# y of the later MoE spans by seven products of halves, half of the relus on ScalarE

## The chip, the cores and the metric

The kernel runs on one core of a Trainium2 chip. The metric is device time in microseconds (us), the median of several runs: 257.5 us before the change (three runs, 256.58 to 257.63).

## What is computed

Blockwise causal attention over 8 batches, 8 heads, 576 positions and a head dimension of 64, and then, over the 4608 tokens of 512 features that it gives, a layer that takes the larger of two projections:

```python
mask = block_i >= block_j            # blocks of 64 positions
attn = softmax(where(mask, scale * q @ k.T, -1e9))
x = (attn @ v)                       # as 4608 x 512
h1, h2 = x @ w1, x @ w2              # 512 -> 1024
out = maximum(h1, h2) @ w_out        # 1024 -> 512
```

The kernel rewrites the second half with max(h1, h2) = h2 + relu(h1 - h2). With d = w1 - w2 and M = w2 @ w_out it computes g = relu(x @ d) and out = x @ M + g @ w_out. M is formed once, on chip. So y, the output, is a product with a contraction of 1536: 4 chunks of 128 rows from x and M, 8 chunks from g and w_out.

## The kernel before

**Attention** goes by head pairs: two heads share the 128 partitions, four pairs make a batch, 32 pairs in all. For a pair, TensorE forms transposed scores in PSUM (the pool `ps_s`, two buffers of two banks), ScalarE takes the exponential into the tile `aT` (`exp`), POOL writes zeros over the masked corners (`mask`), and two pairs later (`LAG`) TensorE multiplies by v (`av`, output `ps_o`, first the query tiles 0 and 1, then 2 to 4). VectorE divides by the sums (a reciprocal and a multiplication into `xp`). `xp` is transposed into `xT`, mostly by DMA. q is transposed on TensorE (`transposes`, two PSUM tiles, one copied out by VectorE, one by ScalarE); from the seventh group on k is transposed by DMA.

**The MoE layer** goes by spans of tokens: two short ones of the first batch (256 and 320 tokens), seven of 512, and a last one of 448. As the spans from the third on begin 64 tokens off a multiple of 128, a span carries the last 64 columns of g over from the one before (a POOL copy at its first h), and its y covers four whole tiles of 128 tokens. For each span there are 8 units `h_unit(i, f)`, each of 4 matmuls of 512 columns and a relu from PSUM into g on VectorE, and 4 units `y_unit(i, s)`, each of 12 matmuls of 512 columns, a copy from PSUM to the tile `y` on VectorE, and a 256 KB store issued by SP. The last tile of the last span is cut into 256, 128 and 128 columns (`y_last`).

**Order.** The scheduling is manual: each engine executes in the order in which the program is written. `plan()` lists the MoE units, `fill(n)` takes n steps from them (a step is one matmul and, at the end of a unit, what follows it), skipping units whose tokens are not yet there. The main loop goes over groups of two pairs and puts fills between the scores, the attention outputs and the transposes. h, y, attention outputs and all transposes share one PSUM pool, `ps_m`, with four buffers of one bank; a new tile takes the buffer that was let go first, and its first matmul waits for the last reader of the tile before.

From the fourth span on the pattern repeats every four pairs: the 8 h units of a span, then its 4 y units, with the attention of four pairs between. The two q transposes of such a cycle stand one in the y part and one where the next h part begins. The last two spans run at the end with no attention beside them.

Of the kernel before, what the change touches and what calls it, by code (L numbers as in the profile page):

```python
# [8 lines left out]
FP32 = mybir.dt.float32  # L9
BF16 = mybir.dt.bfloat16  # L10
AF = mybir.ActivationFunctionType
# [3 lines left out]
def kernel(  # L15
# [10 lines left out]
    nc = tc.nc  # L26

    B, H, S, D = q.shape
    P = 128
# [3 lines left out]
    d_model = H * D  # L33
# [3 lines left out]
    NTOK = B * S  # L37
# [33 lines left out]
    spans = [(0, QCUT), (QCUT, S - QCUT)]  # L71
    spans += [(t0, min(SPAN, NTOK - t0)) for t0 in range(S, NTOK, SPAN)]
    NSPAN = len(spans)


    carry = [t0 % P for t0, _ in spans]
    tiles = [(carry[i] + w) // P for i, (_, w) in enumerate(spans)]

# [5 lines left out]
    wraw = ctx.enter_context(tc.tile_pool(name="wraw", bufs=4))  # L84
    qkn = ctx.enter_context(tc.tile_pool(name="qkn", bufs=2))
    g_pool = ctx.enter_context(tc.tile_pool(name="g", bufs=2))
    y_pool = ctx.enter_context(tc.tile_pool(name="y", bufs=4))
    ps_s = ctx.enter_context(tc.tile_pool(name="ps_s", bufs=2, space=bass.MemoryType.PSUM))
    ps_m = ctx.enter_context(tc.tile_pool(name="ps_m", bufs=4, space=bass.MemoryType.PSUM))

# [9 lines left out]
    xT = ring.tile([P, NDM, NTOK + BLK], BF16, name="xT")  # L100
    d_sb = wpool.tile([P, NDM, d_ff], BF16, name="d_sb")
    bT_sb = wpool.tile([P, NFF, d_model], BF16, name="bT_sb")
    m_sb = wpool.tile([P, NDM, d_model], BF16, name="m_sb")
    wo_sb = wpool.tile([P, NFF, d_model], BF16, name="wo_sb")
# [5 lines left out]
    dve, pool, act = nc.vector.tensor_copy, nc.gpsimd.tensor_copy, nc.scalar.copy  # L110
# [51 lines left out]
    def load_v(b, c):  # L162
        rows = min(P, S - c * P)
        nc.gpsimd.dma_start(  # L164
            out=vv_r[b % NV][P - rows:, c, :, :D],
            in_=v[b, :, c * P:c * P + rows, :].rearrange("h p d -> p h d"),
        )
# [7 lines left out]
    for j in range(d_ff // WB):  # L175
        row, n = (1, j) if j < 3 else (3, 0)
        t0 = 3 * S - 3 * BLK + n * NDM * WB
# [21 lines left out]
    dve, pool, act = nc.vector.tensor_copy, nc.gpsimd.tensor_copy, nc.scalar.copy  # L199
# [28 lines left out]
    g_tiles = {}  # L228

    def h_unit(i, f):  # L230
        if f == 0:
            g_tiles[i] = g_pool.tile([P, NFF, SPAN + BLK], BF16, name="g")
            if carry[i]:
                end = carry[i - 1] + spans[i - 1][1]
                nc.gpsimd.tensor_copy(  # L235
                    out=g_tiles[i][:, :, :carry[i]],
                    in_=g_tiles[i - 1][:, :, end - carry[i]:end])
        g = g_tiles[i]
        t0, w = spans[i]
        m = carry[i]  # L240
        pt = ps_m.tile([P, SPAN], FP32, name="ps_h", tag="m")
        for c in range(NDM):
            nc.tensor.matmul(  # L243
                pt[:, :w], d_sb[:, c, f * P:(f + 1) * P], xT[:, c, t0:t0 + w],
                start=(c == 0), stop=(c == NDM - 1),
            )
            if c == NDM - 1:
                nc.vector.tensor_scalar_max(g[:, f, m:m + w], pt[:, :w], 0.0)  # L248
            yield

    def bT_unit(j):
        pt = ps_m.tile([P, 2, NDM, P], BF16, name="ps_bT", tag="m")
        for i in range(2):
            for c in range(NDM):
                nc.tensor.transpose(pt[:, i, c, :], w2_sb[j][:, c, i * P:(i + 1) * P], ident[:])
                if i == 1 and c == NDM - 1:
                    (act if j % 2 else dve)(
                        out=bT_sb[:, 2 * j:2 * j + 2, :],
                        in_=pt.rearrange("p i c d -> p i (c d)"))
                yield  # L260
# [19 lines left out]
    def y_unit(i, s):  # L280
        t0 = spans[i][0] - carry[i] + s * P
        py = ps_m.tile([P, d_model], FP32, name="ps_y", tag="m")
        terms = y_terms(i, s)
        for n, (lhs, rhs) in enumerate(terms):
            nc.tensor.matmul(  # L285
                py[:], lhs, rhs, start=(n == 0), stop=(n == len(terms) - 1),
            )
            if n == len(terms) - 1:
                y = y_pool.tile([P, d_model], FP32, name="y")
                nc.vector.tensor_copy(out=y[:], in_=py[:])  # L290
                nc.sync.dma_start(out=out[t0:t0 + P, :], in_=y[:])
            yield

    def y_last(i, s):
        t0 = spans[i][0] - carry[i] + s * P
        for m, w, copy, queue in ((0, 256, act, SP), (256, P, dve, SP), (384, P, act, ACT)):
            py = ps_m.tile([P, w], FP32, name="ps_y", tag="m")
            terms = y_terms(i, s)
            for n, (lhs, rhs) in enumerate(terms):
                nc.tensor.matmul(  # L300
                    py[:], lhs, rhs[:, m:m + w], start=(n == 0), stop=(n == len(terms) - 1),
                )
                if n == len(terms) - 1:
                    y = y_pool.tile([P, d_model], FP32, name="y")
                    copy(out=y[:, :w], in_=py[:])  # L305
                    queue.dma_start(out=out[t0:t0 + P, m:m + w], in_=y[:, :w])
                yield


    units = []  # L310
    NY = NDM + NFF

    def plan():
        def h(i, f):
            t0, w = spans[i]
            units.append((h_unit(i, f), t0 + w, w / SPAN, NDM))

        def y(i, s, last=False):
            t0, w = spans[i]
            if last:  # L320
                units.append((y_last(i, s), t0 + w, 0.333, 3 * NY))
            else:
                units.append((y_unit(i, s), t0 + w, 1.0, NY))

        for i in range(NSPAN):
            for f in range(NFF):
                h(i, f)
                if i == 0 and f % 2:
                    units.append((bT_unit(f // 2), 0, 0.25, 2 * NDM))
                if i > 2 and f % 2 == 0 and f // 2 < tiles[i - 1]:  # L330
                    y(i - 1, f // 2)
            if i == 1:
                for n in range(2 * NDM):
                    units.append((m_unit(n // NDM, n % NDM), 0, 0.5, NFF))
                for j in range(2):
                    for s in range(tiles[j]):
                        y(j, s)
        n = tiles[-1]
        for s in range(n):
            y(NSPAN - 1, s, s == n - 1)  # L340

    plan()
    todo = [[n, u, need, cost] for u, need, cost, n in units]
# [225 lines left out]
    def pool_work(s):  # L569
        g, i = divmod(s, 2)  # L570
        if s == 4:
            load_qk(4, (SP, SP), gated=True)
        elif s == 5:
            load_qk(5, (SP, SP), gated=True)
            cast("q", 4, ((pool, 0, RPP),))
            cast("k", 4, ((pool, 0, RPP),))
        else:
            if i == 1 and g + 3 < NG:
                load_qk(g + 3, (SP, SP), gated=True)
            if i == 1 and g + 2 < NG:  # L580
                cast("q", g + 2, ((pool, 0, RPP),))
                cast("k", g + 2, ((pool, 0, RPP),))
            nb, j = divmod(s + 2, HP)
            if nb < B:
                for c in ((0, 1), (2, 3), (4,), ())[j]:
                    load_v(nb, c)
            for nm in "qk":
                if i == 1 and g + 3 < NG and by_dma(nm, g + 3):
                    load_blocks(nm, g + 3)
# [112 lines left out]
    n = fill_of(GPB)  # L702
# [10 lines left out]
    for g in range(GPB + 1, NG):  # L713
        a, b = 2 * g, 2 * g + 1
        old = done_tokens[0]
        if x_due:
            x_out(x_due.pop())
        n, new = fill_of(g), done_tokens[0]
        region(tile_0(a), tile_1(a))
        lo, hi = max(3, n // 18), n * 2 // 9  # L720
        for p, tiles in ((a, lambda: (tile_2(a), tile_0(b))), (b, lambda: (tile_1(b), tile_2(b)))):
            done_tokens[0] = old if p == a and x_by_dma(g - 2) else new
            fill(hi)
            av_with(p - LAG, lo)
            done_tokens[0] = new
            if p % 2 and x_by_dma(g - 1):
                x_dma(g - 1)
            if p % 2 == 0:
                for nm in "qk":
                    if g + 1 < NG and by_dma(nm, g + 1):  # L730
                        transpose_blocks(nm, g + 1)
            copy_out = t_pair(p)
            outs = tiles()
            copy_out()
            region(*outs)
            if p % 2 and g + 1 < NG:
                pad_keys(p + 1)
                pad_keys(p + 2)
            pool_work(p)
        x_due.append(g - 1)  # L740
        fill(n - 2 * (lo + hi))
    for p in range(NPAIR - LAG, NPAIR):
# [48 lines left out]
```

## Time and profile before

| | |
|---|---|
| median of the runs | 257.5 us (256.58 to 257.63) |
| span of the profiled execution, first to last instruction | 255.8 us |
| around the span, by the median | 1.7 us |
| the profiled execution's own time | not listed; the page gives its span |
| mean granted TensorE clock | 1.000 |
| TensorE busy | 245.8 us |
| VectorE busy | 149.9 us |
| ScalarE busy | 120.1 us, none between about 204 and 250 us |
| POOL busy | 128.0 us |
| h matmuls, 320, and y matmuls, 280 + 140 + 36 | 68.3 us and 70.6 + 38.1 us and the end |
| chain that ended last, share of TensorE | 86% |

A group in the profile is a line of the kernel, an engine, an operation and the tiles that it writes and reads, with its count, its busy time, the mean duration of one, and the idle time of the engine in front of it. Matmuls overlap in their pipeline, so the duration of one is longer than the time from one start to the next; the busy time of a group is the union of its instructions.

### The profile page before, as it was taken

The page shows a single profiled execution, that of the slowest core. Times are in us where ns is not written, and L with a number is a line of the kernel's source. Part 1 is how long each engine was busy: PE and PEld are TensorE (multiplying, and loading weights), DVE is VectorE, ACT ScalarE, POOL GpSimd, SP SyncE. Part 2 cuts the span into 40 slices and gives each one's busy share as a digit, 9 for nine tenths or more (in the row PEclk, how much of TensorE's full clock was granted, in tenths as well). Part 3 has the DMA queues.
Part 4 walks back from the last instruction along what each step waited for, and adds up shares of the span by engine and source line. Part 5 has one row for each costly group of instructions (what it writes and reads, how often), then busy time and mean ns, then how long its engine had stood idle before and what let it go on. Part 6 is the DMA issues. An engine that isn't in the chain of part 4 may idle for free.

```text
span 255.8 us, 6863 instructions
## 1 busy us (share of the span) xinstructions
PE 245.8 (96%) x2803; PEld 136.5 (53%) x2803; DVE 149.9 (59%) x320; ACT 120.1 (47%) x159; POOL 128.0 (50%) x294
## 2 busy tenths in 40 slices
PE   8699999899999999999999999999999999999994
PEld 2346767765555555555555555555555554444443
DVE  4876986656576447644764476457544864664521
ACT  2788864477565555555555555555555400000000
POOL 1986951588869457845784578557331200000000
PEclk9999999999999999999999999999999999999999
DMA  6999999599999999999999999999952301202122
GB/s 240 316 222 308 190 265 229 191 127 175 171 144 231 154 219 147 214 138 232 161 197 153 218 166 219 151 216 160 118 103 85 85 23 70 85 0 82 66 100 84
DMA packets 104384, 41.29 MB, mean 161 GB/s; under 512 B 89248, under 2 KB 93728, under 8 KB 104352
## 3 DMA queue, kind: packets, MB, share of 16 engines
q0 software_dynamic: 65952, 11.87, 60.9%
q1 hardware_dynamic: 37984, 28.32, 48.4%
q10 hardware_dynamic: 416, 0.66, 0.8%
q8 instruction: 22, 0.36, 0.7%
q14 instruction: 10, 0.08, 0.1%
HBM read 34.60 MB, written 9.44 MB: 172 GB/s over the span
## 4 chain that ended last, share of the span: by engine, by line
PE 86%; DMA 6%; POOL 3%; ACT 2%; DVE 1%; issue 1%; SPq 0%; POOLq 0%
PE ps_y L285 37%; PE ps_h L243 22%; PE ps_o L507 10%; PE ps_s L399 8%; PE ps_w L369 4%; DMA kraw<-in_k_dram 3%; DMA qraw<-in_q_dram 3%; PE ps_qT L380 2%; PE ps_M L266 1%; ACT aT L423 1%; PE ps_y L300 1%; POOL kn L160 1%; PE ps_s L417 1%; POOL wo_sb L196 1%; PE ps_xe L545 1%
## 5 line engine op out<-in xcount | busy, mean ns | idle before, releaser
L423 ACT ACTIVATE aT<-ps_s 128x1024 bf16<-128x1024 f32 (+2 forms) x100 | 95.7, 994 | 46.1 <-PE ps_s L399 34.2
L285 PE MATMUL ps_y<-wo_sb,g 128*128 128x512 bf16 x280 | 70.6, 380 | 0.0
L243 PE MATMUL ps_h<-xT,d_sb 128*128 128x512 bf16 (+3 forms) x320 | 68.3, 358 | 0.3 <-DVE d_sb L190 0.3
L248 DVE TENSOR_SCALAR g<-ps_h 128x512 bf16<-128x512 f32 (+3 forms) x80 | 50.7, 637 | 17.5 <-PE ps_h L243 15.2
L428 POOL MEMSET aT<- 64x128 bf16 x124 | 22.0, 199 | 60.9 <-ACT aT L423 59.8
L290 DVE COPY y<-ps_y 128x512 f32<-128x512 f32 x35 | 24.2, 692 | 45.9 <-PE ps_y L285 45.0
L243 PEld LDWEIGHTS <-d_sb 128*128 128x128 bf16 x320 | 29.5, 98 | 30.1 <-issue 2.3
L507 PEld LDWEIGHTS <-aT 128*128 128x128 bf16 x960 | 37.2, 98 | 13.5 <-issue 0.8
L285 PEld LDWEIGHTS <-g 128*128 128x128 bf16 x280 | 24.9, 98 | 30.7 <-issue 5.3
L507 PE MATMUL ps_o<-vv,aT 128*128 128x65 bf16 x960 | 39.8, 194 | 0.0
L285 PE MATMUL ps_y<-m_sb,xT 128*128 128x512 bf16 x140 | 38.1, 379 | 0.0
L164 POOL DMA_DIRECT2D vv<-in_v_dram x40 | 34.0, 857 | 1.3 <-issue 0.9
L399 PE MATMUL ps_s<-qT,kT 64*128 64x64 bf16 (+6 forms) x344 | 31.2, 280 | 1.6 <-ACT kT L388 0.7
L514 DVE TENSOR_TENSOR xp<-ps_o,rec 128x256 bf16<-128x256 f32 (+1 forms) x64 | 31.4, 491 | 2.2
L137 POOL DMA_DIRECT2D kb<-in_k_dram x40 | 29.4, 759 | 0.0
L513 DVE RECIPROCAL rec<-ps_o 128x4 f32<-128x4 f32 (+1 forms) x64 | 11.9, 186 | 23.7 <-PE ps_o L507 23.5
L305 ACT COPY y<-ps_y 128x256 f32<-128x256 f32 (+1 forms) x2 | 0.6, 318 | 48.4 <-PE ps_y L300 48.4
L388 ACT COPY qT<-ps_qT 128x576 bf16<-128x576 bf16 (+1 forms) x17 | 10.3, 613 | 27.2 <-PE ps_qT L380 27.2
L160 POOL CAST qn<-qraw 128x1152 bf16<-128x1152 f32 (+1 forms) x16 | 17.0, 1061 | 8.4 <-DMA qraw<-in_q_dram 8.4
L285 PEld LDWEIGHTS <-xT 128*128 128x128 bf16 x140 | 12.8, 98 | 13.1 <-issue 0.4
L399 PEld LDWEIGHTS <-kT 64*128 64x128 bf16 x344 | 12.0, 94 | 11.6 <-issue 6.2
L235 POOL COPY g<-g 128x512 bf16<-128x512 bf16 x8 | 4.9, 613 | 22.4 <-DVE g L248 22.1
(58 smaller groups left out, 152.1 us busy)
## 6 DMA issues: line engine op xcount, KB each, us to landing
qraw<-in_q_dram SPq DMA_DIRECT2D x16, 576.0 KB, 4.9
out_dram<-y SPq DMA_DIRECT2D x35, 256.0 KB, 4.1
vv<-in_v_dram POOLq DMA_DIRECT2D x32, 128.0 KB, 5.6
kraw<-in_k_dram SPq DMA_DIRECT2D x5, 576.0 KB, 7.5
kb<-in_k_dram POOLq DMA_DIRECT2D x40, 72.0 KB, 6.4
w1raw<-in_moe_w_dram POOLq DMA_DIRECT2D x4, 512.0 KB, 7.4
xT<-in_moe_w_dram POOLq DMA_DIRECT2D x4, 256.0 KB, 7.9
wo_sb<-in_moe_w_out_dram POOLq DMA_DIRECT2D x2, 512.0 KB, 10.2
```

What stands on the lines that cost most here:

```text
L137: nc.gpsimd.dma_start(out=n[h * BLK:(h + 1) * BLK, :, s], in_=(q if nm == "q" else k)[b, 4 * u + 2 * s + h].rearrange("(j p) d -> p j d", ...
L160: copy(out=n[:, j0:j1], in_=t[:, j0:j1])
L164: nc.gpsimd.dma_start(out=vv_r[b % NV][P - rows:, c, :, :D], in_=v[b, :, c * P:c * P + rows, :].rearrange("h p d -> p h d"),)
L243: nc.tensor.matmul(pt[:, :w], d_sb[:, c, f * P:(f + 1) * P], xT[:, c, t0:t0 + w], start=(c == 0), stop=(c == NDM - 1),)
L248: nc.vector.tensor_scalar_max(g[:, f, m:m + w], pt[:, :w], 0.0)
L285: nc.tensor.matmul(py[:], lhs, rhs, start=(n == 0), stop=(n == len(terms) - 1),)
L290: nc.vector.tensor_copy(out=y[:], in_=py[:])
L399: nc.tensor.matmul(ps[:, hh, col:col + w], kT[r, k0:k0 + P], qT[r, q0:q0 + w], start=True, stop=True,)
L423: nc.scalar.activation(out=aT_r[p % NA][:, :, a0:a0 + w], in_=ps[:, :, :w], func=AF.Exp, scale=scale,)
L428: (eng or nc.gpsimd).memset(aT_r[p % NA][BLK:, :, a0:a0 + BLK], 0.0)
L507: nc.tensor.matmul(po[:, gi, hh, :], a[:, hh, a0:a0 + P], vv[:, c, h0 + 2 * hh, :], start=(mm == 0), stop=(mm == n_mm - 1),)
L514: nc.vector.tensor_mul(xp[:, :, ts[0]:ts[0] + n, p % 2].rearrange("q s t d -> q t s d"), po[:, :, :, :D], rec[:, :n].to_broadcast([P, n, 2 ...
```

## The change

From the fourth span on (`i >= FAST`, `FAST = 3`) the four y tiles of a span are no longer formed one by one. The 512 tokens, the contraction of 1536 and the 512 output features are each cut in two, and the 2 x 2 by 2 x 2 product of halves is formed by seven products instead of eight (Strassen's scheme in Winograd's form). A product takes 256 tokens, a contraction of 768 (2 chunks of x, 4 of g) and 256 features: 12 matmuls of 256 columns, six for each 128 tokens, into one PSUM bank.

- The right sides are halves of (M, w_out) or one of four sums of them. `weight_sums(n)` forms these once, in eight steps on VectorE, one after each of the pairs 10 to 17, in the four buffers that held w1.
- The left sides are halves of (x, g) or one of four sums of them. `row_sums` forms these on VectorE for every span: the x part behind the relus of f = 2, 4, 5 and 6, the g part (into `bT_sb`, free by then) ahead of products 1 and 6.
- `after` combines the products: product 1 is copied out of PSUM by ScalarE, the others are added by VectorE to fp32 tiles in SBUF. Each quarter of the output leaves by one store of 256 rows of 1 KB; in the last span the quarter of product 2 goes in three.
- The products of a span stand in the order 1, 2, 6, 5, 4, 7, 3 among the h units of the next span in the plan; those of the last span in the order 1, 4, 6, 5, 7, 3, 2.
- From the fourth span on the relus with odd f, and all of the last two spans, are done by ScalarE.
- The pool `y` has six buffers instead of four.

```diff
+    FAST = 3
...
-    y_pool = ctx.enter_context(tc.tile_pool(name="y", bufs=4))
+    y_pool = ctx.enter_context(tc.tile_pool(name="y", bufs=6))
...
             if c == NDM - 1:
-                nc.vector.tensor_scalar_max(g[:, f, m:m + w], pt[:, :w], 0.0)
+                if i >= FAST and on_act(i, f):
+                    nc.scalar.activation(out=g[:, f, m:m + w], in_=pt[:, :w], func=AF.Relu)
+                else:
+                    nc.vector.tensor_scalar_max(g[:, f, m:m + w], pt[:, :w], 0.0)
+                if i >= FAST and f in X_SUMS:
+                    row_sums(i, X_SUMS[f], 0)
...
+    def weight_sums(n):
+        m, op, x, y = (
+            (1, sub, (0, 1), (0, 0)), (3, sub, (1, 1), (0, 1)),
+            (2, add, 3, (0, 0)), (4, sub, (1, 0), 2))[n // 2]
...
+        op(t_parts(m)[n % 2], get(x)[n % 2], get(y)[n % 2])
+
+    def row_sums(i, n, k):
+        op, x, y = (
+            (add, (1, 0), (1, 1)), (sub, 1, (0, 0)), (sub, (0, 0), (1, 0)), (sub, (0, 1), 2))[n - 1]
+        get = lambda z: a_parts(i, *z) if isinstance(z, tuple) else s_parts(i, z)
+        op(s_parts(i, n)[k], get(x)[k], get(y)[k])
...
+    G_SUMS = {1: (1, 2), 6: (4, 3)}
+    X_SUMS = {2: 1, 4: 2, 5: 3, 6: 4}
+
+    def on_act(i, f):
+        return i >= 8 or f % 2
+
+    def product(i, n, cuts=((0, 0, HN), (1, 0, HN))):
+        for m in G_SUMS.get(n, ()):
+            row_sums(i, m, 1)
...
+            for c in range(6):
+                nc.tensor.matmul(
+                    pt[:, q0:q0 + w], lhs[c][:, s * P:(s + 1) * P], rhs[c][:, m:m + w],
+                    start=(c == 0 and q0 == 0), stop=(c == 5 and q0 + w == pt.shape[1]),
+                )
+                if c == 5 and q0 + w == pt.shape[1]:
+                    after(i, n, st, pt, p0, q0 + w)
+                yield
+
+    def after(i, n, st, pt, p0, w):
...
+        if n == 1:
+            st["u"] = new()
+            act(out=st["u"][:], in_=pt[:])
+        elif n == 2:
+            if i < NSPAN - 1:
+                st["c"] = new()
+                add(st["c"][:], pt[:], st["u"][:])
...
+            store(st["c"], 0, 0)
+        elif n == 6 and i < NSPAN - 1:
+            add(st["u"][:], pt[:], st["u"][:])
...
+        elif n == 5:
+            st["v"] = new()
+            add(st["v"][:], pt[:], st["u"][:])
+            if 4 in st:
+                add(st["u"][:], st[4][:], st["u"][:])
+        elif n == 4:
+            if "v" in st:
+                add(st["u"][:], pt[:], st["u"][:])
+            st[4] = pt
+        elif n == 7:
+            t = new()
+            add(t[:], pt[:], st["v"][:])
+            store(t, 1, 1)
+            add(st["u"][:], pt[:], st["u"][:])
+            store(st["u"], 1, 0)
+        elif n == 3:
+            add(st["v"][:], pt[:], st["v"][:])
+            store(st["v"], 0, 1)
+
+    ORDER = (1, 2, 6, 5, 4, 7, 3)
+    LAST = (1, 4, 6, 5, 7, 3, 2)
...
                 h(i, f)
+                if i > FAST and f < 7:
+                    units.append((product(i - 1, ORDER[f]), spans[i - 1][0] + spans[i - 1][1], 0.5, NY))
...
-                if i > 2 and f % 2 == 0 and f // 2 < tiles[i - 1]:
+                if 2 < i <= FAST and f % 2 == 0 and f // 2 < tiles[i - 1]:
                     y(i - 1, f // 2)
...
-        n = tiles[-1]
-        for s in range(n):
-            y(NSPAN - 1, s, s == n - 1)
+        for n in LAST:
+            units.append((product(NSPAN - 1, n, ((0, 0, HN), (1, 0, P), (1, P, P))) if n == 2 else
+                          product(NSPAN - 1, n), NTOK, 0.5, 18 if n == 2 else NY))
...
             pool_work(p)
+            if 0 <= p - 10 < 8:
+                weight_sums(p - 10)
```

## The prediction

> **What bounds the kernel now.** I read the busy shares first, then the slices of the span, the groups of instructions, the busy time by window, and last the timeline of each engine inside one repeating cycle.
>
> ```profile
> span 255.8 us, 6863 instructions
> PE 245.8 (96%) x2803; PEld 136.5 (53%) x2803; DVE 149.9 (59%) x320; ACT 120.1 (47%) x159; POOL 128.0 (50%) x294
> PE   8699999899999999999999999999999999999994
> ...
> L285 PE MATMUL ps_y<-wo_sb,g 128*128 128x512 bf16 x280 | 70.6, 380 | 0.0
> ```
>
> Next, busy time by engine in two windows of 12.73 us (PE, weight loads, VectorE, ScalarE, POOL, then granted clock, DMA share, GB/s):
>
> ```profile
> 98.86:111.59 12.73, 12.73 (x150) 6.80 (x147) 8.10 (x17) 7.01 (x10) 9.77 (x21) 1.00 1.66 171
> 111.59:124.32 12.73, 12.73 (x151) 6.80 (x147) 6.53 (x15) 7.01 (x10) 6.99 (x18) 1.00 1.56 193
> ```
>
> TensorE is busy in every slice between the first and the last ones, and the y matmuls never find it idle (last column 0.0). The two windows are the halves of a cycle of 25.46 us: four head pairs, 32 h matmuls and 48 y matmuls, one MoE span. In it VectorE works 14.63 us and ScalarE 14.02, at the full granted clock. So TensorE's issue rate is the bound, and what matters is the start-to-start time of a matmul, not its 380 ns duration. The timeline (start, length, x count) gives it:
>
> ```profile
> 242.49 1.89 PE L285 MATMUL ps_y<-wo_sb,g 128*128 128x512 bf16 x8
> 47.45 1.48 PE L266 MATMUL ps_M<-wo_sb,bT_sb 128*128 128x256 bf16 x12
> ```
>
> Eight matmuls of 512 columns take 1.89 us; less the last one's 0.379 that is 1.511 / 7 = 215.9 ns each. Twelve of 256 columns: (1.48 - 0.273) / 11 = 109.7 ns, each with its own weight load of 98 ns, hidden.
>
> **What goes and what comes on TensorE.** Seven spans (3 to 9) change. A span's y was 48 x 215.9 = 10.36 us; now it is 7 products x 12 matmuls of 256 columns, 84 x 109.7 = 9.21 us. Gain 1.15 us a span, 8.04 us in all, if no matmul waits longer.
>
> A rule stands against this. The Trainium skill (TensorE: Matmul & The Clock Gate, Back-to-back issue gap) gives a sustained spacing of load-and-matmul pairs of about 81 ns at 128 columns and 131 ns at 512. On a line between them 256 columns would be about 98 ns, an estimate from that page: 84 x 98 against 48 x 131 makes the change lose 1.9 us a span. The same section's N / 2.4 + 2.5 ns gives 109 and 216, which are this trace's rows, so I stay with the rows.
>
> **What comes on the other engines, per span.** VectorE loses four relus (690 ns, L248) and four y copies (692 ns, L290): -5.5 us. It gains seven additions of a PSUM tile into an fp32 tile, 128x512. No row has one; the closest, the division into xp, takes 424 ns for 256 and 557 for 384 columns, so 690 for 512: +4.8. It gains eight sums of rows, bf16 from SBUF, four of 512 and four of 1024 elements. The nearest row is the weight difference L190, 1024 elements in 1215 ns, so 4 x 690 + 4 x 1215 = 7.6; from below, not under eight times the 424 ns of the 256-column division, 3.4. I take 7.6, from the row of the same size. VectorE's cycle becomes 14.63 - 5.5 + 4.8 + 7.6 = 21.5 us of some 24.3.
>
> By the Trainium skill (VectorE: DVE Perf Modes, the perf-mode tier table) tensor_tensor on bf16 in SBUF runs at twice the rate; with its fixed part that would be about 0.69 us for 1024 elements and 4.4 us a span. No row here shows it.
>
> ScalarE gains four relus and one copy a cycle (all eight relus in spans 8 and 9). Its copies take 265 ns for 128 and 372 for 256 columns, so 0.59 for 512: +2.9 us a cycle, 17 of 24.3. In the order of the built kernel ScalarE loads its function table once, as before.
>
> Two averages below one do not say that nothing waits. PSUM has four buffers for h, products, attention outputs and the transposes of q, and the order of the built kernel says whose reader frees which. I walked one cycle with these rows, engine by engine, each instruction starting when its queue and its input allow. Two places are late. For the first, the timelines of TensorE and ScalarE:
>
> ```profile
> 106.78 0.44 PE L380 MATMUL ps_qT<-ident,qn 64*128 64x64 bf16 x18
> ...
> 107.33 0.64 ACT L388 COPY qT<-ps_qT 128x576 bf16<-128x576 bf16 x1 [2.05 <-PE ps_qT L380]
> 107.87 1.03 ACT L423 ACTIVATE aT<-ps_s 128x1024 bf16<-128x1024 f32 x1
> 108.92 0.27 ACT L479 ACTIVATE aT<-ps_s 64x128 bf16<-64x128 f32 x1
> 109.22 1.02 ACT L423 ACTIVATE aT<-ps_s 128x1024 bf16<-128x1024 f32 x1
> ```
>
> First place. ScalarE copies product 1 out of PSUM (u, L411 of the changed kernel), queued behind exactly the four instructions shown. Counted from the q transposes at 106.78, the last exp frees ScalarE at 110.2, the copy ends at 110.8, and the signal arrives at about 110.87. The buffer is wanted by the 24 attention matmuls that come after the 6 transposes and scores (0.83), 16 product matmuls (1.74), 6 attention matmuls (0.20) and 6 more (0.66): 106.78 + 3.43 = 110.21. TensorE waits 0.66 us. Behind the copy, VectorE's addition of product 2 (which needs u) and the two row sums after it are late as well, but still done before products 7 and 3 ask.
>
> Second place. After product 7 VectorE makes two additions (L435, L437), and behind them stands the reciprocal and division of the next attention output, whose buffer the second q transpose takes. From the end of product 7: additions start at 0.2 and follow at 0.61 (690 less the 80 ns overlap that the relu at 104.90 and the reciprocal at 105.51 show), the division ends at 2.06, the signal at 2.12. TensorE is there after 0.20 + 6 x 0.1097 + 0.82 = 1.69. It waits 0.43 us.
>
> The relus of f = 5 and 7, now behind two exps, come out 0.16 and 0.45 us before their buffers are wanted; the sums of rows before products 6 and 5 have over 1 us. Spans 3 to 6 are full cycles: 4 x 0.66 = 2.64. Only three of them have q transposes after product 7: 3 x 0.43 = 1.29. Spans 7 and 8 run with little attention beside them and I find no wait there.
>
> In span 9, with no other work to hide in, product 6 needs two row sums that wait for the last relu: 0.75 + 2 x 1.215 = 3.2 us after the last h, while TensorE is through products 1 and 4 at 2.63: 0.6 us (0 if a sum took the lower bound's 0.424). The stores: before, 256 KB left every 2.59 us; now products 7, 3 and 2 release 1 MB within 2.5 us, in rows of 1 KB instead of 2. Stores took a DMA share of 0.15 over 4 us for 256 KB, so 0.6 us each when packed, twice that if time goes by packets: 2.4 to 4.8 us from the first store 7.5 us after the last h. The last small store is out at about 9.7 and lands in about 2.2. The loss lies between 0 and 1.4; I take 0.4, nearer the end that the byte rate gives.
>
> At nothing: the eight weight sums (4 x 690 + 4 x 1215 = 7.6 us once, on VectorE) fall in pairs 10 to 17, two cycles with 10.8 idle VectorE us each; without that cover they would cost up to 7.6. SP issues as many stores as before; the k and x transposes queued behind them wait at most until the second addition of product 7, 1.5 us after that product, about when the attention matmuls that they also wait for end. Two more y buffers cost no time. POOL's instructions are unchanged.
>
> Sum: 8.04 - 2.64 - 1.29 - 0.6 - 0.4 = 3.1 us. The profiled span becomes 255.8 - 3.1 = 252.7; the median of the runs is 1.7 above the span, so 257.5 - 3.1 = **254.4 us**.
>
> **Rivals.**
> A, no waits: the buffers come free in time, because the copy or the additions are quicker than the rows. Gain 8.04 - 0.4 = 7.6: 249.9. For it: TensorE shows no waits today. Against: the ScalarE chain above is back to back already.
> B, more waits of the same kind: the relu of f = 5 misses its 0.16 us by one exp (0.92), and row sums are held up. 0.8 more in each of four cycles: 3.2, nothing left, 257.6.
> C, slower, VectorE becomes the bound: its in-order queue idles about 2.6 us a cycle waiting for products 5, 4 and 7, so 21.5 + 2.6 = 24.1. If the sums, whose two inputs lie in SBUF, also stand against POOL's copies and casts (two of 1.15, four of 0.27, one of 0.61: 4.0 us a cycle), it is 28.1 against 25.46: four cycles lose 10.6, the other spans gain 2.5, 265.6. It turns slower by 0.5% once a cycle exceeds 26.4, that is when such blocking costs over 2.3 us. Against it: VectorE shows only 1.0 us of waits named after POOL in the relus now, but it has few such sums. The Trainium skill (SBUF — State Buffer, Who interferes with whom) has a lock between a VectorE operation with two SBUF inputs and a GpSimd operation that reads SBUF; nothing shown here tests it.
> D, the products' matmuls do not run at 109.7 ns among other work. The last tile's 256-column matmuls, L300, do. Left inside C.
>
> **How the numbers follow.** Forecast 0.50, A 0.15, B 0.18, C 0.17. Forecast's own range: waits of 0.5 to 1.5 us a cycle, tail loss of 0 to 2: 252 to 256. The forecast and A are faster by over 0.5%, about what this kernel's runs can tell from no change (below 256.2). B is mostly within it, a few in a hundred on either side; C is slower. So faster 0.67, same 0.13, slower 0.20. The range takes A and B: 249.5 to 258.0, leaving out C and a little.
>
> **What would show it.** 84 matmuls of 256 columns a span, starts 110 ns apart; the waits of TensorE naming the u copy (about 0.66 us, four times) and the division behind product 7 (0.4, three times); VectorE between 75 and 90% busy in the cycles; row sums near 1.2 us (or near 0.7); from the last h (241.63) to the end about 14.0 us against 14.2 now. Wrong if TensorE's starts spread, if a wait on the relus of ScalarE leads the list, or if row sums stretch beside POOL's casts.

## The result, and the profile after

The changed kernel takes **253.65 us** (median of four runs, 253.11 to 254.14) against 257.56 for the kernel before on the same chip (four runs, 256.58 to 258.09). The ratio is 0.9845, 95% interval 0.9812 to 0.9877: faster by 1.5%, 3.9 us. The forecast was 254.4. The profiled span fell from 255.8 to 252.2 us. Here and below, a run that took over 1.5% more than the fastest one of its kernel is given apart from the median.

The page of the changed kernel: its span, busy shares, TensorE's row of the slices, and two groups (busy time, mean ns | idle time before them and what ended it).

```profile
span 252.2 us, 7449 instructions
PE 238.7 (95%) x3037; PEld 160.2 (64%) x3037; DVE 172.1 (68%) x371; ACT 143.4 (57%) x200; POOL 129.3 (51%) x294
...
PE   8699899799999999999999999999999999999992
...
L644 PE MATMUL ps_o<-vv,aT 128*128 128x65 bf16 x960 | 39.8, 194 | 1.6 <-ACT y L411 1.6
...
L386 PE MATMUL ps_p<-sums,bT_sb 128*128 128x256 bf16 x168 | 25.2, 273 | 0.0
```

TensorE lost 7.1 us of busy time though it runs 234 matmuls more, and it is still busy in every slice but the first ones and the last. The products themselves never find it idle (0.0). The attention matmuls do now, and they name the u copy on ScalarE, L411. VectorE rose from 59% to 68%, ScalarE from 47% to 57%.

The waits of TensorE (total, times, longest) show the two that the prediction walked out, and no other in the cycles:

```profile
PE ps_o L644 <- ACT y L411: 1.6, 4, 0.4
...
PE ps_qT L517 <- DVE xp L651: 0.7, 3, 0.2
```

These idle times are counted from modelled ends of matmuls, so I read the delay from starts instead. TensorE's timeline at both places, one cycle:

```profile
109.69 0.38 PE L386 MATMUL ps_p<-sums,xsum 128*128 128x256 bf16 x2
110.48 0.90 PE L644 MATMUL ps_o<-vv,aT 128*128 128x65 bf16 x24 [0.40 <-ACT y L411]
...
119.22 0.20 PE L517 MATMUL ps_qT<-ident,qn 64*128 64x64 bf16 x1
119.66 0.43 PE L517 MATMUL ps_qT<-ident,qn 64*128 64x64 bf16 x17 [0.24 <-DVE xp L651]
```

Two matmuls of 256 columns from 109.69 on are issued in 0.22 us, so the attention matmuls could have started at 109.91; they start at 110.48, **0.57 us late**. The second transpose follows the first after 0.44 us where its kind otherwise follows after 0.02: **0.42 us late**. What TensorE waits for the first time, from ScalarE's timeline:

```profile
107.04 0.64 ACT L525 COPY qT<-ps_qT 128x576 bf16<-128x576 bf16 x1 [1.02 <-PE ps_qT L517]
107.57 1.03 ACT L560 ACTIVATE aT<-ps_s 128x1024 bf16<-128x1024 f32 x1
108.63 0.27 ACT L616 ACTIVATE aT<-ps_s 64x128 bf16<-64x128 f32 x1
108.92 1.02 ACT L560 ACTIVATE aT<-ps_s 128x1024 bf16<-128x1024 f32 x1
109.84 0.58 ACT L411 COPY y<-ps_p 128x512 f32<-128x512 f32 x1
```

And the second time, from VectorE's:

```profile
117.76 0.69 DVE L435 TENSOR_TENSOR y<-ps_p,y 128x512 f32<-128x512 f32 x1 [0.62 <-PE ps_p L386]
118.37 0.68 DVE L437 TENSOR_TENSOR y<-ps_p,y 128x512 f32<-128x512 f32 x1
118.97 0.17 DVE L650 RECIPROCAL rec<-ps_o 128x4 f32<-128x4 f32 x1
119.17 0.42 DVE L651 TENSOR_TENSOR xp<-ps_o,rec 128x256 bf16<-128x256 f32 x1
```

ScalarE is back to back from the q copy to the u copy; on VectorE the two additions of product 7 stand in front of the division. Neither queue has a free moment in which the late instruction could have gone earlier, so the waits are set by the order in the queues and not by a shortage of engine time. The busy time of one full cycle (us, then TensorE, weight loads, VectorE, ScalarE, POOL, clock, DMA share, GB/s) shows that:

```profile
105.22:117.85 12.63, 12.23 (x180) 10.03 (x179) 9.57 (x21) 8.29 (x12) 8.37 (x20) 1.00 1.96 153
117.85:130.49 12.64, 12.40 (x153) 7.20 (x150) 9.36 (x20) 8.45 (x12) 8.43 (x20) 1.00 1.44 223
```

The cycle is 25.27 us long (25.46 before), and VectorE works 18.93 us of it, 75%, ScalarE 16.74. A full cycle gained only 0.2 us: 1.19 from the products, less 0.57 and 0.42.

**The account.** By starts of matmuls, a 256-column matmul takes 109.2 ns, and a span's products 1.19 us less than its y. Seven spans: 8.33. Less 4 x 0.57 = 2.28, less 3 x 0.42 = 1.26, less 0.88 at the end of the kernel (below): 3.91 us, which is the measured 3.9. That it agrees to a hundredth is luck: the two profiled spans differ by 3.6, as the changed kernel's profile comes to its first y matmul 0.35 us later (52.62 against 52.27).

At the end of the kernel, first the changed kernel's timeline, VectorE and the queue that issues stores (start, length, and the number of instructions in the group):

```profile
245.86 2.37 SPq L405 DMA_DIRECT2D out_dram<-y  x3
...
247.09 0.96 DVE L417 TENSOR_TENSOR y<-ps_p,y 128x256 f32<-128x256 f32 x3
248.34 1.43 SPq L402 DMA_DIRECT2D out_dram<-y  x3
```

Then the timeline of the kernel before, ScalarE and its queue:

```profile
252.25 0.27 ACT L305 COPY y<-ps_y 128x128 f32<-128x128 f32 x1 [0.97 <-PE ps_y L300]
252.54 0.36 ACTq L306 DMA_DIRECT2D out_dram<-y  x1
```

Before, the last small store left at once, on ScalarE's own queue, when its copy was done. Now all six stores of the last span go through SP's queue: one of them, from 246.46 on, takes 1.26 us to issue, and the last three come about half a microsecond apart. The last one is issued from about 249.4 although its addition ended at 248.05, and the transfers overlap (DMA share 1.01 from 249 to 250 us). From the last matmul to the end of the span it was 3.59 us and is 4.47.

### The profile page after: what moved, and what is told of

It is laid out like the page before. It is cut to its first block, busy times and chain, and to the rows that moved or that the text cites. A ratio compares the mean times of both kernels' runs of the same rounds, so it can differ in the third digit from the quotient of the medians.

```text
span 252.2 us, 7449 instructions
## 1 busy us (share of the span) xinstructions
PE 238.7 (95%) x3037; PEld 160.2 (64%) x3037; DVE 172.1 (68%) x371; ACT 143.4 (57%) x200; POOL 129.3 (51%) x294
## 4 chain that ended last, share of the span: by engine, by line
PE 71%; ACT 10%; DMA 6%; DVE 6%; POOL 3%; issue 2%; SPq 0%; ACTq 0%; DVEq 0%; POOLq 0%
PE ps_p L386 21%; PE ps_h L244 19%; PE ps_y L291 9%; PE ps_o L644 8%; PE ps_s L536 7%; ACT aT L560 6%; PE ps_w L506 4%; DMA kraw<-in_k_dram 4%; DMA qraw<-in_q_dram 3%; DVE bT_sb L360 2%; ACT g L250 2%; PE ps_qT L517 2%; PE ps_M L272 1%; POOL kn L161 1%; DVE y L435 1%
## 5 line engine op out<-in xcount | busy, mean ns | idle before, releaser
L244 PE MATMUL ps_h<-xT,d_sb 128*128 128x512 bf16 (+3 forms) x320 | 69.4, 358 | 0.3 <-DVE d_sb L191 0.3
L252 DVE TENSOR_SCALAR g<-ps_h 128x512 bf16<-128x512 f32 (+2 forms) x44 | 26.4, 605 | 13.6 <-PE ps_h L244 13.1
L250 ACT ACTIVATE g<-ps_h 128x512 bf16<-128x512 f32 (+1 forms) x36 | 20.9, 586 | 23.2 <-PE ps_h L244 22.3
L386 PE MATMUL ps_p<-sums,bT_sb 128*128 128x256 bf16 x168 | 25.2, 273 | 0.0
L386 PEld LDWEIGHTS <-bT_sb 128*128 128x128 bf16 x224 | 21.4, 98 | 3.4 <-issue 1.0
L386 PEld LDWEIGHTS <-g 128*128 128x128 bf16 x172 | 15.6, 98 | 3.5 <-issue 1.9
L386 PE MATMUL ps_p<-wo_sb,g 128*128 128x256 bf16 (+1 forms) x116 | 17.6, 269 | 0.0
L291 PE MATMUL ps_y<-wo_sb,g 128*128 128x512 bf16 x64 | 16.7, 380 | 0.0
L236 POOL COPY g<-g 128x512 bf16<-128x512 bf16 x8 | 5.9, 732 | 20.6 <-ACT g L250 20.3
```

What stands on the lines that cost most here:

```text
L244: nc.tensor.matmul(pt[:, :w], d_sb[:, c, f * P:(f + 1) * P], xT[:, c, t0:t0 + w], start=(c == 0), stop=(c == NDM - 1),)
L250: nc.scalar.activation(out=g[:, f, m:m + w], in_=pt[:, :w], func=AF.Relu)
L291: nc.tensor.matmul(py[:], lhs, rhs, start=(n == 0), stop=(n == len(terms) - 1),)
L386: nc.tensor.matmul(pt[:, q0:q0 + w], lhs[c][:, s * P:(s + 1) * P], rhs[c][:, m:m + w], start=(c == 0 and q0 == 0), stop=(c == 5 and q0 + w ...
```

## The experiments

My theory: TensorE's issue rate is the bound, the products save 1.19 us in each of seven spans, and four waits of 0.57 and three of 0.42, made by the order in two queues, take almost half of it back. Rivals: VectorE is the bound or near it (C); 256-column matmuls cost more among other work (D); the relus on ScalarE have a part in the result.

### The two waits, taken away one by one

Three kernels come from the changed one. In the first, VectorE makes the u copy in the spans that have attention beside them:

```diff
-            act(out=st["u"][:], in_=pt[:])
+            (dve if i < 7 else act)(out=st["u"][:], in_=pt[:])
```

> Product 1 of spans 3 to 6 is copied out of PSUM by VectorE instead of ScalarE; nothing else differs from the changed kernel. Theory (the wait of the attention matmuls on u, 0.57 us in each of four cycles, is ScalarE's queue: the copy stands behind q copy and two exps): VectorE has room in front of the division of the next attention output, the copy is done about 0.4 us before the buffer is wanted, the four waits go, 4 x 0.57 = 2.3 us less: 251.4 us, and no wait of ps_o on the u copy in the profile. The wait behind product 7 (0.42 us, three times) stays. Rival (VectorE is the resource that is short, the wait only moves to whatever VectorE now does later): less than 0.7 us gained, 253.0 to 254, with a new wait on VectorE near the row sums or product 6.

In the second, product 4 comes after product 7, so that product 7's second addition (L437) is no longer ahead of the division; the store of its quarter moves with it:

```diff
         elif n == 4:
             if "v" in st:
                 add(st["u"][:], pt[:], st["u"][:])
+            if 7 in st:
+                store(st["u"], 1, 0)
...
             add(st["u"][:], pt[:], st["u"][:])
-            store(st["u"], 1, 0)
+            st[7] = True
+            if 4 in st:
+                store(st["u"], 1, 0)
...
-    ORDER = (1, 2, 6, 5, 4, 7, 3)
+    ORDER = (1, 2, 6, 5, 7, 4, 3)
```

> Products 7 and 4 change places in the order of spans 3 to 8 (the store of the quarter that product 4 completes moves with it); the same instructions otherwise. Theory (the second q transpose waits because product 7 puts two additions in front of the division whose buffer it takes): with product 4, which has one addition, in that place the division ends 0.6 us earlier, 0.2 us before it is wanted; three waits of 0.42 us go, 1.3 us less: 252.4 us. The waits on the u copy stay at 0.57 us. Rival (the wait is for the attention output itself or for VectorE's load in general): the wait on the division stays within 0.1 us and the time at 253.6.

The third has both edits.

> Both edits: product 1 of spans 3 to 6 copied by VectorE, and products 7 and 4 exchanged. Theory (two separate queues are late, the rest of the gain is there): both kinds of waits go, 2.3 + 1.3 = 3.6 us less than the changed kernel: 250.1 us, cycles of 24.3 us instead of 25.26, TensorE busy without idle time in the cycles. Rival (VectorE is nearly the bound, so that taking waits away brings others): 252 us or more.

Measured, against 257.19 us for the kernel before on the same chip:

| kernel | median (range), us | ratio, 95% interval |
|---|---|---|
| u copy on VectorE | 251.08 (250.72 to 251.48) | 0.9768 (0.973 to 0.9805) |
| product 4 after 7 | 251.98 (251.21 to 252.34) | 0.9795 (0.9761 to 0.9829) |
| both | 250.58 (249.51 to 251.25) | 0.974 (0.9702 to 0.9779) |

Of TensorE's two waits, the kernel with the u copy on VectorE keeps only this one:

```profile
PE ps_qT L517 <- DVE xp L651: 0.7, 3, 0.2
```

and the kernel with product 4 after 7, whose lines have moved by four, only the other:

```profile
PE ps_o L648 <- ACT y L411: 1.6, 4, 0.4
```

The kernel with both edits has neither.

By the ratios the three are 2.0, 1.3 and 2.7 us faster than the changed kernel (0.9845), where I had written 2.3, 1.3 and 3.6; the intervals are about 1 us wide to each side. The medians carry noise from the head of the kernel: the first y matmul starts between 51.89 and 52.62 us in these five profiles. So I compare from there to the first matmul of the last span. In the kernel before these are

```profile
52.27 1.05 PE L285 MATMUL ps_y<-m_sb,xT 128*128 128x512 bf16 x4
...
241.63 1.03 PE L285 MATMUL ps_y<-m_sb,xT 128*128 128x512 bf16 x4
```

and in the kernel with both edits

```profile
52.09 1.05 PE L291 MATMUL ps_y<-m_sb,xT 128*128 128x512 bf16 x4
...
234.30 0.38 PE L386 MATMUL ps_p<-m_sb,xT 128*128 128x256 bf16 x2
```

| | first y to last span, us | against before | against the changed kernel |
|---|---|---|---|
| before | 189.36 | | |
| changed | 185.76 | -3.60 | |
| u copy on VectorE | 183.51 | -5.85 | -2.25 (4 x 0.57 = 2.28) |
| product 4 after 7 | 184.53 | -4.83 | -1.23 (3 x 0.42 = 1.26) |
| both | 182.21 | -7.15 | -3.55 (3.54) |

Six spans lie in this stretch, 6 x 1.19 = 7.14. Without the two waits the whole saving of the products arrives, and each wait is worth what the starts said. The u copy's move put 0.6 us more on VectorE per cycle, on average, and made the kernel faster, which already speaks against C. One full cycle of the kernel with both edits, TensorE busy for all of it and VectorE at 79%:

```profile
104.70:128.96 24.26, 24.26 (x329) 17.13 (x328) 19.08 (x41) 16.28 (x23) 15.88 (x37) 1.00 1.61 180
```

### The relus alone

The kernel before, with the changed kernel's distribution of relus and nothing else:

```diff
-                nc.vector.tensor_scalar_max(g[:, f, m:m + w], pt[:, :w], 0.0)
+                if i >= 3 and (i >= 8 or f % 2):
+                    nc.scalar.activation(out=g[:, f, m:m + w], in_=pt[:, :w], func=AF.Relu)
+                else:
+                    nc.vector.tensor_scalar_max(g[:, f, m:m + w], pt[:, :w], 0.0)
```

> The kernel before, with only the other half of the change: the odd relus from the fourth span on, and all of the last two spans, on ScalarE. y is formed as before. Theory (TensorE's issue rate is the bound and relus wait for nobody before): within 0.3% of the kernel before, 257.5 us, busy time moved from VectorE to ScalarE (36 relus, 22 us). Rival (moving the relus is itself a gain, or a loss because they stand behind exps): more than 1 us from it either way.

257.61 us (257.13 to 258.27, ten runs), ratio 1.0014, interval 0.9997 to 1.0032: no effect that can be told from none. The move of the relus alone is worth nothing.

### The MoE work without attention

To see the products without the attention's queues I took the attention out of both kernels: x is read from q as it lies, and the rest (folding of the weights, h, y or products, stores) stays. In the changed kernel the eight sums of weights then come together, ahead of the first products. The core of the edit:

```diff
+    qx = q.rearrange("b h s d -> (b h s d)").rearrange("(p c t) -> p c t", p=P, c=NDM)
+    for b in range(B):
+        nc.gpsimd.dma_start(out=xT[:, :, b * S:(b + 1) * S], in_=qx[:, :, b * S:(b + 1) * S])
...
+    done_tokens[0] = NTOK
+    while total - left() < 32 + 32 + 32 + 64 + 12 * (tiles[0] + tiles[1]) + 32:
+        fill(1)
+    for n in range(8):
+        weight_sums(n)
+    fill(100000)
```

> The kernel before without its attention: x is read from q as it lies, in eight transfers, the weights are loaded and folded as before, and only the MoE work is left (so the output is not the reference's). It is the base for the three kernels beside it, and no theory hangs on its own time: a full span should take 32 + 48 matmuls of 512 columns, 80 x 215.9 ns = 17.3 us, with TensorE waiting for nothing.

> The changed kernel without its attention, in the same way (x read from q as it lies; the eight sums of weights are formed before the third span's products). There are no scores, exponentials or divisions between the products here, so neither of the two waits that I name can exist. My theory: it gains 1.19 in each of seven spans, 8.3, less 0.9 that the stores at the end take back: 7.4 us under the kernel before without attention, between 6.6 and 8.2; a span takes 16.1 instead of 17.3. Of the full kernel's missing gain, the waits are then the reason. Rival C (VectorE bounds the span): with only MoE work a span is shorter, VectorE works some 13 us of it, and if its sums and additions decide, the gain is under 5 here as well. Rival D (matmuls of 256 columns cost more among other work): the same 4 us as in the full kernel.

Without attention the kernel before takes 195.03 us (194.71 to 196.44; ratio to the full kernel before 0.7602, interval 0.7561 to 0.7643), the changed one 189.05 (188.55 to 189.53; 0.7355, 0.7329 to 0.7381). That is 5.98 us less, where I had written 6.6 to 8.2. The starts say where the rest is. TensorE's timeline of the kernel before without attention, two y tiles one span (four tiles) apart:

```profile
138.06 1.03 PE L204 MATMUL ps_y<-m_sb,xT 128*128 128x512 bf16 x4
...
155.33 1.03 PE L204 MATMUL ps_y<-m_sb,xT 128*128 128x512 bf16 x4
```

and of the changed one, product 1 of two spans in a row:

```profile
94.95 0.38 PE L305 MATMUL ps_p<-m_sb,xT 128*128 128x256 bf16 x2
...
111.03 0.27 PE L305 MATMUL ps_p<-m_sb,xT 128*128 128x256 bf16 x1
```

A span takes 17.27 us before and 16.08 after, 1.19 less, with no wait of TensorE in the spans of either; from the first y matmul (42.21 and 43.40) to the last matmul's end (190.10 and 182.97) the change gains 147.89 - 139.57 = 8.32 us, seven times 1.19. Of that, the end of the kernel takes back 1.3 (3.1 us from the last matmul to the end before, 4.4 after), and the head 1.2 in this profile: TensorE waits 17.9 us for the first x instead of 16.2, and is longer at half clock (mean granted clock from 26 to 30 us 0.63 against 0.83). The head spreads, the first y matmul starting at 42.2 to 43.6 us in the six kernels of this kind, and I have no cause for it. The saving itself is there in full: this excludes D, and it agrees with the first experiments that in the full kernel the two waits are what is missing.

### How much VectorE can carry

These three kernels, too, are without attention. None of their edits was measured in the full kernel, so what they show of VectorE's room is shown for the MoE work alone.

First, each of the four g row sums of a span made twice, the second writing the same values:

```diff
         for m in G_SUMS.get(n, ()):
             row_sums(i, m, 1)
+            row_sums(i, m, 1)
```

> The changed kernel without attention, with each of the four g row sums of a span done twice (the second writes the same values; the attention is left out in the same way): 2.75 us more VectorE work per span, about what the row sums would cost at the 1.2 us that my sum used for them. VectorE then has some 15.7 us of a span of 16.1. My theory, TensorE as the bound: the spans grow by less than 0.3, and the sums of the last span stand in front of its product 6 and cost up to 1.4 us: 0.5 to 3 us more than the changed kernel without attention. Rival C: every span grows by most of 2.75, over 10 us more.

190.48 us (189.93 to 190.88; ratio 0.7409, 0.7384 to 0.7435), 1.4 more than without the doubled sums. The full spans did not move at all, with VectorE at 85% (13.69 us; I had written 15.7, but without the second sums it is 11.11 and not 13):

```profile
111.10:127.18 16.08, 16.08 (x118) 11.35 (x116) 13.69 (x23) 2.98 (x5) 0.61 (x1) 1.00 0.20 66
```

Most of the loss is in the last span, where product 6 now waits for its sums (0.8 us by the waits, 1.1 by the starts; the rest lies in the head and the end, which differ by 0.1 and 0.4 in the two profiles):

```profile
PE ps_p L306 <- DVE bT_sb L279: 0.8, 1, 0.8
```

So this is what my price of 1.2 us for a sum of 1024 elements would have meant, had it been right: a wait in the last span and, without attention beside them, nothing in the spans.

Then all the relus back on VectorE, the sums made once:

```diff
     def on_act(i, f):
-        return i >= 8 or f % 2
+        return False
```

> The changed kernel without attention (left out in the same way, output not the reference's) with all relus back on VectorE: the second half of the change undone alone. VectorE works 11.0 us of a 16.1-us span there; four relus of 0.62 make it 13.5. My theory, TensorE as the bound: the cycles do not move; the last span had all its eight relus on ScalarE, so its sums come later behind them: 189.05 plus 0 to 1.0. The rival, that ScalarE's half of the relus is what makes room for the sums: over 2.5 us more in each of seven spans.

189.43 us (188.78 to 189.99; ratio 0.7352, 0.7286 to 0.7419), no difference that can be told from 189.05. VectorE works 13.79 us of the same 16.08. With the products, too, the half of the relus on ScalarE gains nothing here; in the full kernel this is not shown.

At last both, and each g row sum three times:

```diff
             row_sums(i, m, 1)
+            row_sums(i, m, 1)
+            row_sums(i, m, 1)
...
-        return i >= 8 or f % 2
+        return False
```

> The same with all relus on VectorE and each g row sum done three times (the copies write the same values; attention left out in the same way): 5.5 us more again, VectorE busy for some 19 us of a span of 16.1, 17 to 18 if neighbouring instructions overlap by a tenth, as additions that start every 0.61 us and last 0.69 do. It looks for the point at which the rival C begins. Now C must come true: each of seven spans 1 to 3 us longer, 7 to 20 us in all; if the spans still do not grow, VectorE's busy time is no measure of its room at all.

218.6 us (218.55 to 220.6 in three runs, a fourth took 222.14; ratio 0.8512, 0.8426 to 0.8598): 29.2 us more than with the sums made once, and more than the 7 to 20 that I had written. Two spans in a row:

```profile
119.42:138.89 19.47, 16.41 (x118) 11.24 (x116) 18.67 (x32) 0.59 (x1) 0.62 (x1) 1.00 0.16 55
138.89:160.03 21.14, 18.09 (x118) 11.95 (x116) 18.85 (x32) 0.59 (x1) 0.62 (x1) 0.92 0.15 50
```

C is real: 13.8 us of VectorE's work in a span of 16.08 cost nothing, 18.7 make the span 19.5. Where between the two it begins is not shown. I had allowed for neighbours that overlap; the tripled sums do not (three take 2.14 us, 0.71 each). And some spans are longer still, 21.1, at a granted clock of 0.92; the last section shows why.

### The stores at the end

In the same kernel without attention, with both edits of the first experiments, the last span's products in the order 1, 2, 6, 5, 3, 7, 4, the last one cut in three, and the last piece's store on ScalarE's queue:

```diff
-    LAST = (1, 4, 6, 5, 7, 3, 2)
+    LAST = (1, 2, 6, 5, 3, 7, 4)
...
-                nc.sync.dma_start(
+                (ACT if p0 + w == d_model else SP).dma_start(
```

> The changed kernel without attention (left out in the same way), with the two mends, and with the last span's products in the order 1, 2, 6, 5, 3, 7, 4, so that its four quarters of the output leave one product (1.31 us) apart, the last product cut in three and its last piece's store issued from ScalarE's queue. My theory: the end is the transfers of quarters that become ready together (4.5 us from the last matmul to the end, against 3.6 before the change), so spreading them brings it back to 3.5 to 4.0: 0.5 to 1.0 us less than the changed kernel without attention. The rival, that the end is the fixed path of the last addition and the last transfer: no change, within 0.3.

188.04 us (187.45 to 189.16 in three runs, a fourth took 190.32); ratio 0.7323, 0.7283 to 0.7362, which overlaps with 0.7355 (0.7329 to 0.7381). Inconclusive: it is 1.0 us less, as the theory would have it, but its runs spread by more than that. The only profile is of the run that took 190.32 us and says nothing of the other three. Whether spreading the quarters is worth anything stays open.

## Why the prediction was right, and where not

**The bound and the gain.** TensorE's issue rate was and is the bound. The price of a span, 1.15 us, was 1.19 (1.31 us for twelve matmuls, 109.2 ns each, where I had 109.7): 8.33 instead of 8.04. Against the rows stood the rule of the Trainium skill (TensorE: Matmul & The Clock Gate, Back-to-back issue gap) that a stream of load-and-matmul pairs sustains 81 ns at 128 and 131 ns at 512 columns. These streams, each matmul with its own weight load, take 109.2 ns at 256 columns and 215.9 at 512, and the cuts of 128 columns at the end start 55 ns apart; the rule's estimate of a loss of 1.9 us a span did not come true, and the change gained.

**The first wait.** Forecast 0.66 us four times behind the queue of four ScalarE instructions; measured 0.57 four times, behind the same four. Counted from the q transposes, TensorE asked for the buffer after 3.43 us, as walked (106.48 to 109.91), and got it after 4.00 where I had 4.09. Right.

**The second wait.** Forecast 0.43 three times, measured 0.42 three times, behind product 7's two additions. An addition takes 0.69, as estimated from the division's rows. Right.

**The sums of rows: the step that failed.** I took 1.215 us for 1024 elements, from the row of the same size, the difference of weights. They take 0.688, and 512 elements 0.415 instead of 0.69. The row that I used, from the kernel before, and a row of the sums, from the changed kernel (shortest, median, longest in ns):

```profile
L190 DVE TENSOR_TENSOR d_sb<-w1raw,xT x4: 1215/1215/1215, 17.6 to 31.2; 128x1024 bf16<-128x1024 f32 x4
...
L360 DVE TENSOR_TENSOR bT_sb<-g x14: 682/688/694, 106.1 to 241.3; 128x1024 bf16<-128x1024 bf16 x14
```

The first has an fp32 tile among its inputs, and the sums are bf16 throughout: the row agreed in size and not in type (no run changes the type alone). The lower value that I gave by the Trainium skill (VectorE: DVE Perf Modes, the perf-mode tier table), 0.69 from its double rate for bf16, is what the trace shows. With it the 0.6 us wait of product 6 in the last span falls away: the second sum ends at 240.64 and product 6 starts at 241.0. The doubled sums brought this very wait back, so its mechanism was right and the size of the sum was wrong.

**The end.** The 0.4 us (0 to 1.4) for stores was 0.88: mis-sized within its bounds. I had left out that stores on one queue are issued half a microsecond apart, and that the last small store, ScalarE's before, is SP's now: I had it out 9.7 us after the last h, and it is issued after 11.0. How much of the 0.88 this makes is not shown; the kernel that spread the stores was inconclusive. From the last h to the end I had 14.0 us against 14.2; it is 13.82 against 14.17.

The errors partly cancel: 0.3 more gain, 0.4 less waiting, 0.6 that did not come, 0.5 more at the end make 0.8 us, and the forecast was 0.75 too high. That it came this close is in part luck.

**The rivals.** A (no waits, 249.9) names the true gain and fails on the two waits; the kernel with both edits, 250.58, comes close to it. B (more of them) did not come: the relus and the sums are in time. C was too dear by its sums: VectorE works 70 to 75% of a full cycle, without attention 85% still cost nothing, and the blocking by POOL is small (last section). D is excluded by the pitch: 1.19 less in every span without waits.

**The signs that I named.** Row sums came out near 0.7 and not near 1.2, where I had named both. VectorE is at or below the lower edge of the 75 to 90% that I had given it: 75% in the cycle shown, 70 to 72% in the next three. And row sums do stretch beside POOL's casts, which I had named as a sign of being wrong; but no wait of TensorE names these sums.

## What to carry to other kernels

Where one engine is saturated, an edit that shortens its work is worth what the saved instructions cost, less the waits that new readers put in front of its buffers, and these can be walked out beforehand from the in-order queue of each reader; twice here the walk came within 0.1 us. Cost every eviction that you add by the instruction that stands in front of it in its queue and by who gets the buffer next, and then put it on the queue that is empty at that moment: moving one copy and exchanging two products doubled what was left of the gain in the cycles. A row of the trace is a price only for the same types: same size with another input type was wrong by 1.8 times.

## What the runs showed of the hardware

**VectorE's sums and POOL's casts hold each other up, but little.** The sums of x, 512 elements of bf16 from SBUF, in the changed kernel (instructions: shortest, median, longest in ns):

```profile
L360 DVE TENSOR_TENSOR xsum<-xsum,xT x4: 415/636/858, 102.6 to 232.2; 128x512 bf16<-128x512 bf16 x4
...
L360 DVE TENSOR_TENSOR sums<-sums,xT x3: 415/426/856, 127.9 to 217.5; 128x512 bf16<-128x512 bf16 x3
```

and in the kernel without attention, where POOL has no casts:

```profile
L279 DVE TENSOR_TENSOR xsum<-xsum,xT x4: 415/416/417, 71.0 to 167.5; 128x512 bf16<-128x512 bf16 x4
...
L279 DVE TENSOR_TENSOR sums<-sums,xT x3: 415/416/417, 88.4 to 151.8; 128x512 bf16<-128x512 bf16 x3
```

One of the long ones, in the changed kernel's timeline:

```profile
127.30 1.16 POOL L161 CAST qn<-qraw 128x1152 bf16<-128x1152 f32 x1
127.88 0.86 DVE L360 TENSOR_TENSOR sums<-sums,xT 128x512 bf16<-128x512 bf16 x1
```

The sum is issued 0.58 us into the cast and ends at 128.74, 0.28 after the cast, as if it had begun only near the cast's end. Its duration doubles, 0.42 to 0.86. This agrees with the Trainium skill (SBUF — State Buffer, Who interferes with whom), where a VectorE instruction with two SBUF inputs and a GpSimd instruction that reads SBUF contend for a shared read interface. POOL is held up as well: a copy (L236) that takes 0.617 us took 1.08 beside two sums, at 205.85. In both kernels with the u copy on VectorE one sum is issued at nearly the same moment as a cast and takes 1.4 us. In the one without the other edit:

```profile
175.96 1.15 POOL L161 CAST qn<-qraw 128x1152 bf16<-128x1152 f32 x1
175.98 1.39 DVE L360 TENSOR_TENSOR sums<-sums,xT 128x512 bf16<-128x512 bf16 x1
```

So the price was 0.45 us for one sum in a cycle of the changed kernel, and 1.0 us at most in these. My rival C had supposed 4 us a cycle.

**A wait of TensorE can cost more than its length.** In the kernel with tripled sums TensorE waits 2.5 us for an addition that stands behind six sums, in each of six spans. During or just after four of these waits it fell to half clock. One of them in TensorE's timeline:

```profile
106.96 1.03 PE L163 MATMUL ps_h<-xT,d_sb 128*128 128x512 bf16 x4
110.52 0.59 PE L307 MATMUL ps_p<-sums,xT 128*128 128x256 bf16 x2 [2.54 <-DVE y L341]
110.90 1.06 PE L307 MATMUL ps_p<-sums,g 128*128 128x256 bf16 x4
111.75 0.63 PE L307 MATMUL ps_p<-sums,xT 128*128 128x256 bf16 x2
```

and in the windows of the same kernel (the granted clock stands before the DMA share):

```profile
110.50:112.00 1.50, 1.48 (x8) 1.04 (x8) 1.50 (x3) 0.00 (x0) 0.00 (x0) 0.50 0.00 0
...
114.00:115.00 1.00, 1.00 (x10) 0.80 (x9) 0.59 (x1) 0.00 (x0) 0.00 (x0) 1.00 0.00 0
```

Four matmuls of 256 columns take 0.85 us, 212 ns each instead of 109, until about 113.5: some 1.6 us on top of the 2.5, which is the difference between spans of 19.5 and 21.1. After the other two waits of the same length the matmuls kept their 109 ns. The Trainium skill (TensorE: Matmul & The Clock Gate, Part 1: The HAM clock gate) puts the fall to half clock at an idle window of about 3.4 us; here 2.5 us was enough in four of six cases. The waits of 0.57 and 0.42 us in the changed kernel never lowered it.
